# A planned kernel of attention and two feed-forward layers: strided masks on SyncE's queue, a planner that counts eight transfers, three more raw-weight buffers, other constants

## The chip, the cores and the metric

The program runs on one core of one Trainium2 chip. The metric is the device time of one execution in microseconds (us); the median of several runs is quoted. The profile below is of one further execution, which has a time of its own.

## The reference

Attention over 4 batches, 8 heads, 576 positions, head size 64. Heads 0 to 3 use a local mask (a window of 32), heads 4 to 7 a strided mask (every 32nd position). Its output, 2304 tokens by 512, goes through two feed-forward layers of width 2048, all in float32:

```python
mask_local = (rel >= 0) & (rel < stride)                          # stride 32
mask_strided = (rel >= 0) & (pos[None, :] % stride == pos[:, None] % stride)
scores = np.where(masks, scale * q @ k.T, -1e9)
attn = softmax(scores) @ v          # then (B*S, H*D) = (2304, 512)
h = x @ w_in;  g = h * np.clip(h + 3.0, 0.0, 6.0) / 6.0;  x = g @ w_out      # first layer
h = x @ w_in;  g = h * np.tanh(softplus(h));              x = g @ w_out      # second layer
```

The weights reach the chip as raw 64-bit words, from which the kernel makes float32.

## The kernel before

**Attention** goes by 16 pairs of heads (4 batches, 4 pairs). Of each pair a qk tile and a v tile are loaded. TensorE makes the scores (L609), DVE adds the mask out of `mk_loc` or `mk_str` (L622), and the softmax follows: maximum on DVE (L654), subtraction on DVE or POOL (L655), exponential on ACT (L656), sum on DVE (L657), a guard (L661 or L663), reciprocal (L666), and the scaling (L667). TensorE then transposes (L676, L678), ACT or DVE copies the result to `pt`, and TensorE makes the values (L715, 72 rows of the profile to a pass). Before that a part of v has been copied to other partitions (L575 on ACT). The first pairs use the late ends of the `xs` tiles as buffers, which is why some of their loads are named `xs`.

**The feed-forward layers** are matmuls of three products each, high and low parts of both operands (L1012 to L1014). Part of the first layer is done plainly, as soon as attention has some tokens ready; the rest, and most of the second, goes by a seven-product scheme in which sums and differences of blocks take the place of one product in eight.

**Weights** come as 64 loads of 512 KB into `raw` tiles (L793), each then turned into float32 by five DVE passes (L797 to L822, or L830 as the last), the first of which may run on ACT for the first 20. A raw tile is free again after the last pass. The differences of weight blocks (`w<-w`, L898) run on DVE or POOL; a split into high and low part follows (L348 on ACT or L350 on DVE, then L776 on DVE or POOL).

**The order** is not written by hand. Every step is an `Op` with its cost on each engine that may run it, the ops that it waits for, and a due time. `Plan.run` walks through an imagined time: it picks the op that can start first (among those within 11 ns the one due first), puts it on its engine, and at the end emits all ops by their imagined start. An op with two possible engines goes to that whose end, cost times `SLOW` plus `BIAS`, comes first. DVE and POOL shut each other out for the ops marked with `lock`. All loads and stores share one imagined engine `dma`, which does one transfer after another; its results count as there 2.1 us after the end. Where TensorE would stand still in the first 60 us of the plan, `fill` puts in matmuls on zeros (L1382, 512 columns of float32) whose results nobody reads. On the chip each engine runs its list in order and waits by semaphores; a filler that is in the list runs, whether the gap is there or not.

Loads and stores are issued on SyncE (SP), but for the seven loads of the strided masks, which are the first instructions on ScalarE's queue (L515). Of these, three bring rows that POOL or DVE then place in the strided mask (L532). `N_RAW` is 2: raw tile n is loaded when the unpacking of n - 2 is done (L788 and the load below it).

Of the kernel before, what the change touches and what calls it, by code (L numbers as in the profile page):

```python
# [10 lines left out]
U64 = mybir.dt.uint64  # L11
# [4 lines left out]
P = 128  # L16
# [39 lines left out]
N_KEEP = 2  # L56
N_RAW, N_WA, N_T, N_F = 2, 2, 3, 4
N_S = {"c": 2, "u": 2, "v": 2}
N_QKV, N_E, N_PT = 2, 4, 2

ABS_ON_ACT = 20
# [12 lines left out]
ORIGIN = 600  # L74
START, FIRST_PACE = 42920, 3359
UNIT = 858
MASKS_DUE = 1000
# [6 lines left out]
HALF_PACE = 4685  # L84
EARLY_W, EARLY_G, EARLY_X = 10496, 10545, 13159
OVERLAP = 14375
UNIT_Y, UNIT_X = 6429, 15237
LEAD = 1.0667


BIAS = {"act": -305, "dve": 318, "pool": 0}
FIRST_BIAS = {"act": -795, "dve": 929, "pool": -68}
BIAS_FROM = 17386

SLOW = {"pe": 1.0, "act": 1.04, "dve": 1.11, "pool": 0.95, "dma": 1.25}

# [38 lines left out]
class Plan:  # L135
# [84 lines left out]
    def run(self):  # L220
# [11 lines left out]
        done = []  # L232
        left = len(self.ops)
        while left:
            best = None
            for e, waiting in ready.items():
                mine = []
                for item in waiting:
                    r, op = item
# [3 lines left out]
                    t = at[e]  # L243
                    if e == "pe":
                        t += self.late(t, op)
                    if len(op.costs) > 1:
                        bias = BIAS if t > BIAS_FROM else FIRST_BIAS
                        end = {x: at[x] + c * SLOW[x] + bias[x] for x, c in op.costs.items()}
                        if min(end, key=end.get) != e:
                            continue  # L250
# [4 lines left out]
                t, due, item = min((x for x in mine if x[0] <= soon), key=lambda x: x[1])  # L255
# [10 lines left out]
            op.start, op.end = t, self.stream(t, op) if e == "pe" else t + op.cost * SLOW[e]  # L266
            free[e] = op.end
            if e == "pe":
                n = self.counted[-1][0]
                self.counted.extend([(n, t), (n + (op.count or 6), op.end)])  # L270
# [51 lines left out]
def attention_then_two_ffns(ctx, tc, qkv, masks, wts, out):  # L322
# [3 lines left out]
    nc = tc.nc  # L326
# [69 lines left out]
    zeros = spare[0][:, 2 * S:][:, :FILL]  # L396
    scratch = ap_.tile([P, 1], F32, name="scratch")

    def open_late():
# [86 lines left out]
    def load_masks(local):  # L486
# [26 lines left out]
        def load(rows, to, col, dims):  # L513
            src = bass.AP(tensor=masks.tensor, offset=masks.offset + n_mk + col, ap=[*dims, [row, QN], [1, WK]])
            return add("act", 430, lambda: nc.scalar.dma_start(to(rows), src), due=MASKS_DUE)  # L515

# [7 lines left out]
        for h in range(2):  # L524
            done.append(load(halves[h], lambda rows: mk_str[rows, 0], (NB - 1) * SK, [[QN * row + ODD_LAST, 2]]))
        done = [add("dma", 300, lambda: None, done)]
        odd = add("dma", 300, lambda: None, odd)

# [6 lines left out]
        for part in parts:  # L535
            done.append(add(None, {"dve": 200, "pool": 400}, lambda eng, part=part: place(eng, *part), [odd], lock=("dve",)))
        return done
# [226 lines left out]
    for k in halves[::-1]:  # L764
        t = h_due[k] = min(h_due[k] - EARLY_W, t - HALF_PACE)
    raw_ops, wa_ops, w32_ops = [], [], []
    in_use, out_use = {}, {}
# [14 lines left out]
    def unpack(m, fp, k, whole_tile):  # L782


        n = len(raw_ops)
        raw, a = raw_t[n % N_RAW], wa_t[n % N_WA]
        words = raw.bitcast(U32).rearrange("p (n t) -> p n t", t=2)
        low, high = words[:, :, 0], words[:, :, 1]  # L788
        ai = a.bitcast(U32)
        old = raw_ops[n - N_RAW] if n >= N_RAW else []  # L790
        old_a = wa_ops[n - N_WA] if n >= N_WA else []
# [27 lines left out]
        if whole_tile:  # L819
# [4 lines left out]
            )  # L824
            raw_ops.append([o])
            return o, a
        to = w32[:, 4 * (k % 2):][:, :4].bitcast(U32).rearrange("p b c -> p (b c)")
# [4 lines left out]
        )  # L832
        raw_ops.append([o])
        wa_ops.append([o])
        return o
# [622 lines left out]
```

## Time and profile before

| | us |
|---|---|
| median of 3 runs | 824.23 (824.16 to 824.65) |
| the profiled execution | 822.89 |
| its span, first to last instruction | 821.1 |
| busy: TensorE (PE) | 808.3 |
| busy: VectorE (DVE) | 676.0 |
| busy: ScalarE (ACT) | 447.2 |
| busy: GpSimd (POOL) | 325.9 |
| mean granted TensorE clock | 0.997 |

An engine's busy time is a share of the span; matmuls overlap each other in TensorE's pipeline, so that the sum of their durations is more than the busy time. Fillers count as busy. "SPq" and "ACTq" are the instructions by which SyncE and ScalarE issue transfers; they count as busy for no engine.

### The profile page before, as it was taken

How to read it: one execution, taken by the hardware profiler on the slowest of the kernel's cores; microseconds unless marked ns; L12 is line 12 of the kernel's file. 1: busy time of each engine (PE TensorE's matmuls, PEld its weight loads, DVE VectorE, ACT ScalarE, POOL GpSimd, SP SyncE). 2: the span in 40 equal slices, each digit the busy share in tenths (PEclk: the TensorE clock that was granted, in tenths of full speed). 3: DMA queues.
4: the chain of work that ended last, by engine and by line, in shares of the span. 5: the costliest groups of instructions: out<-in, count | busy, mean ns of one | idle time of the engine just before them, and what ended most of it. 6: DMA issues, size and time to landing. Idle time of an engine off the chain costs nothing.

```text
span 821.1 us, 17043 instructions
## 1 busy us (share of the span) xinstructions
PE 808.3 (98%) x6650; PEld 771.0 (94%) x6650; DVE 676.0 (82%) x1238; ACT 447.2 (54%) x941; POOL 325.9 (40%) x324
## 2 busy tenths in 40 slices
PE   6999999999999999999999999999999999999998
PEld 3678888899999999999999999999999999999998
DVE  4888887898999857867889899776888999998766
ACT  2767767666654434434436568556555545545542
POOL 4443421412252314231424324422677456476223
PEclk9999999999999999999999999999999999999999
DMA  8786751477678866765866446665667667765732
GB/s 241 229 248 184 211 178 54 146 303 268 249 251 297 295 251 238 263 226 184 288 219 229 184 168 268 225 239 196 241 240 244 225 212 244 247 237 188 246 126 96
DMA packets 47588, 182.31 MB, mean 222 GB/s; under 512 B 6036, under 2 KB 15380, under 8 KB 47508
## 3 DMA queue, kind: packets, MB, share of 16 engines
q1 hardware_dynamic: 46848, 181.06, 64.0%
q8 instruction: 52, 0.85, 0.4%
q10 hardware_dynamic: 660, 0.16, 0.1%
q14 instruction: 28, 0.23, 0.1%
HBM read 138.74 MB, written 42.47 MB: 221 GB/s over the span
## 4 chain that ended last, share of the span: by engine, by line
PE 89%; DVE 4%; DMA 3%; ACT 1%; POOL 1%; issue 1%; ACTq 0%; SPq 0%; DVEq 0%
PE bank L1012 29%; PE bank L1013 28%; PE bank L1014 28%; PE bank L715 2%; DMA raw<-in_wts_dram 1%; PE bank L609 1%; DMA v<-in_qkv_dram 1%; PE bank L676 1%; DMA mk_str<-in_masks_dram 1%; POOL w L898 1%; PE bank L1382 0%; DMA qk<-in_qkv_dram 0%; DVE wa L816 0%; DVE xs L1295 0%; DVE wa L811 0%
## 5 line engine op out<-in xcount | busy, mean ns | idle before, releaser
L1012 PE MATMUL bank<-x,win 128*128 128x384 f32 (+3 forms) x668 | 227.8, 341 | 0.4 <-POOL win L776 0.2
L1013 PE MATMUL bank<-x,win 128*128 128x384 f32 (+3 forms) x668 | 226.2, 339 | 0.1
L1014 PE MATMUL bank<-x,win 128*128 128x384 f32 (+3 forms) x668 | 226.1, 338 | 0.0
L1012 PE MATMUL bank<-g,wout 128*128 128x384 f32 (+3 forms) x512 | 175.7, 343 | 0.0
L1013 PE MATMUL bank<-g,wout 128*128 128x384 f32 (+3 forms) x512 | 174.2, 340 | 1.1 <-DVE g L776 1.1
L1014 PE MATMUL bank<-g,wout 128*128 128x384 f32 (+3 forms) x512 | 174.0, 340 | 0.0
L1295 DVE TENSOR_TENSOR xs<-bank,xs 128x384 f32<-128x384 f32 x174 | 95.2, 552 | 49.5 <-PE bank L1014 48.3
L1012 PEld LDWEIGHTS bank<-x,win 128*128 128x128 f32 x668 | 125.4, 188 | 5.3 <-POOL win L776 1.4
L1013 PEld LDWEIGHTS bank<-x,win 128*128 128x128 f32 x668 | 125.4, 188 | 2.8 <-POOL x L776 0.5
L1014 PEld LDWEIGHTS bank<-x,win 128*128 128x128 f32 x668 | 125.4, 188 | 2.2
L1013 PEld LDWEIGHTS bank<-g,wout 128*128 128x128 f32 x512 | 96.1, 188 | 3.0 <-DVE g L776 1.1
L1014 PEld LDWEIGHTS bank<-g,wout 128*128 128x128 f32 x512 | 96.1, 188 | 2.3
L1012 PEld LDWEIGHTS bank<-g,wout 128*128 128x128 f32 x512 | 96.1, 188 | 2.0
L898 POOL TENSOR_TENSOR w<-w 128x256 f32<-128x256 f32 x80 | 68.2, 871 | 70.1 <-DVE w L830 69.0
L1013 PE MATMUL bank<-g_late,wout 128*128 128x384 f32 x204 | 68.1, 334 | 0.0
L1012 PE MATMUL bank<-g_late,wout 128*128 128x384 f32 x204 | 68.1, 334 | 0.0
L1014 PE MATMUL bank<-g_late,wout 128*128 128x384 f32 x204 | 68.1, 334 | 0.0
L776 POOL TENSOR_TENSOR x<-xs,x 128x512 fp32r<-128x512 f32 (+3 forms) x17 | 21.1, 1244 | 63.7 <-ACT x L348 52.9
L816 DVE SCALAR_TENSOR_TENSOR wa<-raw,wa 128x512 uint32<-128x512 uint32 x64 | 45.8, 723 | 0.3
L776 POOL TENSOR_TENSOR win<-w,win 128x256 fp32r<-128x256 f32 (+1 forms) x25 | 29.1, 1170 | 40.6 <-ACT win L348 34.9
L348 ACT CAST win<-w 128x512 fp32r<-128x512 f32 (+1 forms) x56 | 31.6, 567 | 22.8 <-DVE w L830 14.6
L348 ACT COPY u<-bank 128x384 f32<-128x384 f32 x42 | 20.2, 482 | 37.6 <-PE bank L1014 37.4
(139 smaller groups left out, 1481.6 us busy)
## 6 DMA issues: line engine op xcount, KB each, us to landing
x<-kept_s SPq DMA_DIRECT2D x60, 768.0 KB, 4.4
x<-kept_a SPq DMA_DIRECT2D x45, 768.0 KB, 4.6
raw<-in_wts_dram SPq DMA_DIRECT2D x64, 512.0 KB, 5.0
kept_s<-x SPq DMA_DIRECT2D x24, 768.0 KB, 3.4
kept_a<-x SPq DMA_DIRECT2D x18, 768.0 KB, 4.0
qk<-in_qkv_dram SPq DMA_DIRECT2D x14, 576.0 KB, 5.3
v<-in_qkv_dram SPq DMA_DIRECT2D x14, 432.0 KB, 5.0
keep<-y SPq DMA_DIRECT2D x24, 192.0 KB, 4.1
```

Of the source, the lines that this page charges most:

```text
L348: nc.scalar.copy(out, src)
L609: nc.tensor.matmul(banks[both[h].n][g * QN:(g + 1) * QN, slot * WK:(slot + 1) * WK], src.q[h * D:(h + 1) * D, n // 6, n % 2 * QN:(n % 2 + ...
L676: nc.tensor.transpose(banks[turned[0].n][:, j * P:(j + 1) * P], e[:, t:t + 2].rearrange("p s k -> p (s k)"), ident)
L715: nc.tensor.matmul(o[h * D:(h + 1) * D], src.v[rows, NB + others(local).index(n) if n in others(local) else i, h * D:(h + 1) * D], pt[rows ...
L776: lambda eng: engines[eng].tensor_tensor(lo(), src(), hi().bitcast(F32), ALU.subtract),
L816: lambda: nc.vector.scalar_tensor_tensor(ai, high, 0xC0000000, ai, ALU.bitwise_and, ALU.bitwise_or),
L898: lambda eng: engines[eng].tensor_tensor(of[out], of[x], of[y], ALU.subtract), [*on[x], *on[y]], lock=("dve", "pool"),
L1012: nc.tensor.matmul(o, low_w, high, start=first, stop=False, skip_group_check=True)
L1013: nc.tensor.matmul(o, high_w, low, start=False, stop=False, skip_group_check=True)
L1014: nc.tensor.matmul(o, high_w, high, start=False, stop=last, skip_group_check=True)
L1295: "dve", dve_ns(n), lambda: nc.vector.tensor_tensor(y(), src(), y(), ALU.add), [prev, y_sums[key]], due=due, frees=frees,
```

## The change

Four edits. The seven loads of strided masks are issued by SyncE and planned on the `dma` engine. The planner lets a transfer start only when the eighth transfer before it has landed. Three more raw tiles serve weight loads number 2, 3, 4 and 7, so that of the first eight loads five need no freed tile. And a number of constants are others. The code's lines shift by 3 to 11 (L609 becomes L615, L715 becomes L721, L1382 becomes L1393, L898 becomes L909).

```diff
+N_RAW_MORE, RAW_EARLY = 3, 8
+LANES = 8
-START, FIRST_PACE = 42920, 3359
+START, FIRST_PACE = 42920, 3750
-EARLY_W, EARLY_G, EARLY_X = 10496, 10545, 13159
+EARLY_W, EARLY_G, EARLY_X = 10496, 10545, 11906
-UNIT_Y, UNIT_X = 6429, 15237
+UNIT_Y, UNIT_X = 5251, 15237
-BIAS = {"act": -305, "dve": 318, "pool": 0}
+BIAS = {"act": -305, "dve": 115, "pool": 45}
-SLOW = {"pe": 1.0, "act": 1.04, "dve": 1.11, "pool": 0.95, "dma": 1.25}
+SLOW = {"pe": 1.0, "act": 1.04, "dve": 1.11, "pool": 0.9037, "dma": 1.2274}
...
+                    elif e == "dma" and len(landed) >= LANES:
+                        t = max(t, landed[-LANES])
...
+            if e == "dma":
+                landed.append(op.end + self.AFTER[e])
...
+    raw_t.extend(ap_.tile([P, DM], U64, name=f"raw_more{k}") for k in range(N_RAW_MORE))
...
-            return add("act", 430, lambda: nc.scalar.dma_start(to(rows), src), due=MASKS_DUE)
+            return add("dma", 400, lambda: nc.sync.dma_start(to(rows), src), due=MASKS_DUE)
...
-        done = [add("dma", 300, lambda: None, done)]
-        odd = add("dma", 300, lambda: None, odd)
...
-        raw, a = raw_t[n % N_RAW], wa_t[n % N_WA]
+        slot = n % (N_RAW + N_RAW_MORE) if n < RAW_EARLY else n % N_RAW
+        raw, a = raw_t[slot], wa_t[n % N_WA]
...
-        old = raw_ops[n - N_RAW] if n >= N_RAW else []
+        old = raw_last.get(slot, [])
```

What this does to the order shows first on SyncE, at the very start of the program. The names are the tiles that are loaded: `mk` the local masks, `mk_str` and `mk_odd` the strided ones, then qk and v tiles of the first pairs. Before:

```order
L489 DMA mk<-in_masks_dram 128x320
L547 DMA qk_143<-in_qkv_dram 128x1152
L547 DMA qk_144<-in_qkv_dram 128x1152
L547 DMA xs_75<-in_qkv_dram 128x1152
L559 DMA v_145<-in_qkv_dram 96x1152
L547 DMA xs_76<-in_qkv_dram 128x1152
L559 DMA v_145<-in_qkv_dram 64x128
L793 DMA raw_79<-in_wts_dram 128x512
```

And now, on the same engine at the same place:

```order
L497 DMA mk<-in_masks_dram 128x320
L523 DMA mk_str<-in_masks_dram 128x1x64 x2
L523 DMA mk_odd<-in_masks_dram 64x1x64 x2
L523 DMA mk_odd<-in_masks_dram 128x1x64
L523 DMA mk_str<-in_masks_dram 64x1x64 x2
L553 DMA qk_143<-in_qkv_dram 128x1152
L553 DMA qk_144<-in_qkv_dram 128x1152
L553 DMA xs_75<-in_qkv_dram 128x1152
L565 DMA v_145<-in_qkv_dram 96x1152
L565 DMA v_145<-in_qkv_dram 64x128
L800 DMA raw_79<-in_wts_dram 128x512
```

Seven mask loads stand ahead of the first qk load; the order behind them is nearly the old one.

ScalarE at the start of the program, before (`e_147` and `e_148` are the scores of the first two pairs, `v_145` the first v tile, `sum_155` the first pair's sums):

```order
L515 DMA mk_str<-in_masks_dram 128x1x64 x2
L515 DMA mk_odd<-in_masks_dram 64x1x64 x2
L515 DMA mk_odd<-in_masks_dram 128x1x64
L515 DMA mk_str<-in_masks_dram 64x1x64 x2
L1381 ACT_TABLE_LOAD
L1381 ACTIVATE scratch<-xs_75 128x1
L656 ACTIVATE e_147<-e_147 128x320
L575 COPY v_145<-v_145 32x1024
L656 ACTIVATE e_147<-e_147 128x256
L661 ACTIVATE sum_155<-sum_155 128x5
```

And now:

```order
L1392 ACT_TABLE_LOAD
L1392 ACTIVATE scratch<-xs_75 128x1
L662 ACTIVATE e_147<-e_147 128x320
L662 ACTIVATE e_147<-e_147 128x256
L581 COPY v_145<-v_145 32x1024
L667 ACTIVATE sum_155<-sum_155 128x5
```

The issues are gone, and the second exponential of the first pair has moved ahead of the copy of v.

TensorE up to the first scores, before (fillers are the rows with 512 columns, `bank` is where a result goes):

```order
L1382 MATMUL bank_61<-xs_75 128x512
L1382 MATMUL bank_62<-xs_75 128x512
L609 MATMUL bank_63<-qk_143 32x64
L609 MATMUL bank_64<-qk_143 32x64
```

And now:

```order
L1393 MATMUL bank_61<-xs_75 128x512
L1393 MATMUL bank_62<-xs_75 128x512
L1393 MATMUL bank_63<-xs_75 128x512
L1393 MATMUL bank_64<-xs_75 128x512
L1393 MATMUL bank_65<-xs_75 128x512
L615 MATMUL bank_66<-qk_143 32x64
L615 MATMUL bank_67<-qk_143 32x64
```

Three more fillers stand ahead of the first scores. In the whole program 24 fillers stand where 17 did, all ahead of the sixth pass of values; by then 30 matmuls of 512 columns stand where 27 did, and seven passes of scores where eight did. Beyond the start, DVE has 104 instructions more (1344 for 1240) and POOL 89 fewer (240 for 329); 50 of the 80 differences `w<-w` are on DVE, where none was. By groups of four, those of the fourth group are all on DVE now, of the last group one.

## Rows read from the trace of the kernel before

**Rows 1.** Windows: length, busy time and instructions by engine, granted clock, transfers' share and GB/s.
```profile
0.00:52.50 52.50, 45.53 (x1065) 28.69 (x1065) 35.64 (x83) 31.96 (x68) 23.12 (x40) 0.97 0.80 237
52.50:60.00 7.50, 6.54 (x166) 5.34 (x166) 6.72 (x13) 3.15 (x7) 5.20 (x4) 1.00 0.82 242
60.00:140.00 80.00, 80.00 (x1558) 67.86 (x1557) 64.38 (x120) 56.21 (x116) 23.47 (x21) 1.00 0.55 167
```

**Rows 2.** Windows of 60 us; first engine PE, then PEld, DVE, ACT, POOL.
```profile
260.00:320.00 60.00, 59.80 (x344) 59.29 (x343) 46.70 (x87) 25.49 (x53) 16.98 (x16) 1.00 0.74 267
380.00:440.00 60.00, 60.00 (x348) 60.00 (x348) 53.06 (x99) 26.69 (x56) 22.04 (x23) 1.00 0.68 233
440.00:500.00 60.00, 59.19 (x342) 58.87 (x341) 51.96 (x96) 37.03 (x81) 20.95 (x20) 1.00 0.51 201
740.00:800.00 60.00, 59.49 (x342) 58.88 (x341) 44.01 (x82) 30.63 (x64) 22.83 (x22) 1.00 0.57 188
```

**Rows 3.** Timeline of PE: start, length, instruction, count, [idle before, and until what].
```profile
1.45 3.50 PE L1382 MATMUL bank<-xs 128*128 128x512 f32 x4 [1.45 <-DVE xs L1380]
5.72 1.05 PE L609 MATMUL bank<-qk 64*32 64x64 f32 x76 [0.77 <-DMA qk<-in_qkv_dram]
...
8.40 3.70 PE L1382 MATMUL bank<-xs 128*128 128x512 f32 x8
...
15.91 1.05 PE L609 MATMUL bank<-xs 64*32 64x64 f32 x76 [2.50 <-DMA xs<-in_qkv_dram]
...
19.00 4.04 PE L1382 MATMUL bank<-xs 128*128 128x512 f32 x6
...
52.50 0.90 PE L715 MATMUL bank<-pt,v 64*64 64x32 f32 x48
```

**Rows 4.** Groups by line, 0 to 60 us: the fillers; busy us, mean ns.
```profile
L1382 PE MATMUL bank<-xs 128*128 128x512 f32 x34 | 19.0, 692 | 1.5 <-DVE xs L1380 1.5
```

**Rows 5.** Timeline of the two issuing queues, 0 to 8 us.
```profile
0.73 1.77 ACTq L515 DMA_DIRECT2D mk_str<-in_masks_dram  x2
1.19 0.97 SPq L547 DMA_DIRECT2D qk<-in_qkv_dram  x2
2.53 1.68 ACTq L515 DMA_DIRECT2D mk_odd<-in_masks_dram  x3
5.09 1.88 ACTq L515 DMA_DIRECT2D mk_str<-in_masks_dram  x2
...
7.08 0.33 SPq L547 DMA_DIRECT2D xs<-in_qkv_dram  x1
...
7.45 0.43 SPq L559 DMA_DIRECT2D v<-in_qkv_dram  x1
```

**Rows 6.** Waits of SyncE's queue, 0 to 60 us: us in total, times, longest.
```profile
SPq L793 <- DVE wa L822: 16.8, 4, 7.6
...
SPq L547 <- DMA mk_str<-in_masks_dram: 4.9, 1, 4.9
```

**Rows 7.** Timelines of ACT and of DVE around 15 us.
```profile
14.45 1.04 ACT L575 COPY v<-v 32x1024 f32<-32x1024 f32 x1 [4.58 <-DMA v<-in_qkv_dram]
...
15.97 0.42 DVE L657 TENSOR_REDUCE sum<-e 128x4 f32<-128x256 f32 x1 [4.86 <-ACT e L656]
```

**Rows 8.** The page's queues: ScalarE's queue; packets, MB, share of 16 engines.
```profile
q10 hardware_dynamic: 660, 0.16, 0.1%
```

**Rows 9.** A window of 3 us; the granted clock is the third number from the end.
```profile
18.50:21.50 3.00, 3.00 (x6) 1.52 (x6) 1.66 (x8) 1.94 (x7) 1.87 (x2) 0.50 0.97 265
```

**Rows 10.** Groups by line: a difference on POOL, and a larger one on DVE.
```profile
L898 POOL TENSOR_TENSOR w<-w 128x256 f32<-128x256 f32 x80 | 68.2, 871 | 70.1 <-DVE w L830 69.0
...
L1237 DVE TENSOR_TENSOR f<-c,u 128x384 f32<-128x384 f32 x7 | 3.9, 557 | 3.0 <-ACT u L1153 3.0
```

**Rows 11.** The chain that ended last: start, us, what; two pieces ahead of late stalls.
```profile
263.83 1.45 POOL w L898 x2
...
743.63 2.97 POOL w L898 x3
```

More of the change, by code (lines that the diff above doesn't have):

```diff
@@ L232, in run @@
         done = []
-        left = len(self.ops)
+        left, landed = len(self.ops), []
         while left:
@@ L535, in load_masks @@
         for part in parts:
-            done.append(add(None, {"dve": 200, "pool": 400}, lambda eng, part=part: place(eng, *part), [odd], lock=("dve",)))
+            done.append(add(None, {"dve": 200, "pool": 400}, lambda eng, part=part: place(eng, *part), odd, lock=("dve",)))
         return done
@@ L765, in attention_then_two_ffns @@
         t = h_due[k] = min(h_due[k] - EARLY_W, t - HALF_PACE)
-    raw_ops, wa_ops, w32_ops = [], [], []
+    raw_ops, wa_ops, w32_ops, raw_last = [], [], [], {}
     in_use, out_use = {}, {}
@@ L825, in unpack @@
             raw_ops.append([o])
+            raw_last[slot] = [o]
+            if slot >= N_RAW:
+                closing.deps.append(o)
             return o, a
@@ L833, in unpack @@
         raw_ops.append([o])
+        raw_last[slot] = [o]
         wa_ops.append([o])
```

## The prediction

> **What bounds the kernel now.** I read the windows first. From 60 us on TensorE is busy throughout: 80.00 of 80.00 us between 60 and 140, and later 60.00 of 60 with 348 matmuls in a window, which is 0.172 us for each [rows 1, 2]. Three later windows hold 344, 342 and 342, so 4 + 6 + 6 = 16 matmuls are missing, and 16 x 0.172 = 2.76 us is all that TensorE loses there. Everything else is lost in the first 60 us: TensorE is busy 45.53 + 6.54 = 52.07 us, so it is idle 7.93 us, 1.45 of it before its first instruction [rows 1, 3]. And 19.0 us of what counts as busy is fillers, the matmuls on zeros of L1382: 34 rows, two to an instruction, so 17 [rows 4]. The time is therefore a fixed amount of matmul work, plus fillers, plus idle time. A faster DVE or POOL is worth nothing unless it removes one of these.
>
> Next I asked why TensorE has nothing to do early. SyncE issues two qk loads by 2.16 us and the next at 7.08; the queue's own waits put 4.9 us of that to a transfer of mk_str [rows 5, 6]. The seven strided-mask loads are ACT's first instructions and take it from 0.73 to 6.97 us. Since SyncE's third load waits for a mask that ScalarE issued, the two queues share a set of semaphores, which the built program's order of waits confirms (eight of them, used in turn). The load of v thus leaves at 7.45 us. ACT's copy of v stands ahead of the second exponential of the first pair; ACT waits 4.58 us for v, and DVE, which needs that exponential, 4.86 us [rows 7]. Later in the first 60 us SyncE stands four times, 16.8 us together, at a raw load whose buffer DVE hasn't freed [rows 6], and all loads behind it wait too.
>
> **The change, part by part.**
> *Masks on SyncE.* ACT loses 1.77 + 1.68 + 1.88 = 5.33 us of issuing. SyncE gains seven issues ahead of the first qk load, from 1.19 us on. What they cost there isn't shown; the bounds are SyncE's shortest row of one issue, 0.33, so 2.3 us, and ACT's 5.33 us [rows 5]. I take 0.45 each, 3.15 us, near SyncE's rows, 0.33 to 0.49. The mask issues would then end at 1.19 + 3.15 = 4.3, and qk leaves at 4.3 in place of 1.19. It lands 4.5 us after issue before (1.19 to 5.72, where TensorE waits for it [rows 3, 5]), so the first scores come at 8.8. Behind qk the 4.9 us wait is gone: the ninth transfer waits for the first one, which landed early. The load of v would leave near 5.8 in place of 7.45.
>
> All 16 transfer engines would need 0.1% of the span, 0.8 us, for the masks' queue [rows 8]. Before, those packets ran on ScalarE's queue beside qk. [...]
>
> *Order of ACT.* Both exponentials now stand ahead of the copy of v, so the stall of 4.86 us on DVE can't come from there again. What is late next is ACT's guard of the sums, which stands behind the copy; with v asked for 1.6 us sooner, that costs less than what was saved.
>
> *Eight transfers under way, and fillers.* The planner now sees loads arrive later, and fills the gaps that it sees: 24 fillers where 17 stood. A filler that stands in a gap costs nothing; one that stands where work is ready delays it. [...] So 24 cost 3.5 + 22 x 0.93 = 24.0 us if the clock doesn't fall again: 5.0 more than the 19.0. Five stand ahead of the first scores and end at 1.45 + 3.50 + 3 x 0.93 = 7.7, so those scores at 8.8 leave 1.1 us idle.
>
> *Three raw buffers.* The third to fifth weight loads need no freed buffer, and SyncE doesn't stand there. The 16.8 us of waiting was not TensorE's own, so I give it no sum of its own; it is why I expect little idle time besides that 1.1.
>
> *Constants.* On POOL the subtraction w (L898) occurs 80 times, 871 ns each; 50 of them move to DVE. DVE's nearest row is 128x384 at 557 ns, 1.5 times the size [rows 10], which is the upper bound; the lower is that in proportion, 371. I take 0.5 us, as fixed costs don't shrink. DVE gets 104 instructions in all, POOL 89 fewer. By 50 x 0.5 and 54 x about 0.6, DVE rises by some 57 us from 676.0 to about 733 of 821 us, and POOL falls by 50 x 0.87 and 39 x about 1.1, to some 240. Engines beside TensorE have that room on average. Two of the three late stalls end in chains with w on POOL: 1.45 us for two, 2.97 us for three [rows 11]. The first group of these is wholly on DVE now, so 1.45 becomes about 1.0; the last keeps three of its four on POOL. The third stall has none. Hence I keep 0.8 of the 2.76 us.
>
> **The sum**, against the profiled execution's own 822.89 us: fillers +5.0; the early idle time, 7.93 - 1.45 = 6.48, goes and 1.6 takes its place (the 1.1 and 0.5 more); late stalls -2.76 + 0.8. That is 5.0 - 6.48 + 1.6 - 2.76 + 0.8 = -1.84, so 821.1. The median of the runs shown, 824.23, is 1.34 above the profiled one, so the forecast is 822.4. In general the change is -4.24 plus the idle time that is left, early and late. With none left it is 820.0. With as much as before (6.48 + 2.76) it is +5.0, thus 829.2: if the plan fills gaps that then open all the same, its fillers are pure loss.
>
> **The rivals.**
> *Everything fits* (idle time 1.1 early and nothing late): -3.1, 821.1. For it: the stalls at 4.9 and 16.8 us of SyncE are real, and the planner now knows them. Against: seven places where a filler ended up in front of ready work need a plan exact to 0.9 us.
> *No change.* Early idle time 2.6, late stalls 1.8: +0.2, 824.4. The gaps only move, because the first scores start 3.1 us later; DVE, now at 733 us, makes new late stalls for those taken away. For it: the stall without w at 440 to 500 us, 6 matmuls, is made of x and g work on DVE, and DVE gets more of both. If the planner's picture of eight transfers isn't the chip's, the change doesn't do what it says, and the result lies here too.
> *Late first scores*, the one on the other side: seven mask issues on SyncE cost as on ACT, 5.33 us. Then qk leaves at 6.5 and lands at 11.0; TensorE has run out of fillers at 7.7, so the gap is 3.3 and not 1.1 us. An idle stretch of 2.50 us was followed by three fillers in 4.04, 1.25 more than 3 x 0.93 [rows 3]. The wait of 2.50 us for an xs load comes again, all transfers being late. 3.3 + 1.25 + 2.5 + 0.8 - 4.24 = +3.6, 827.8. From 5.9 us of idle time in all the kernel is slower by over 0.2%. For it: four of the loads are 128 short rows, and ACT took 0.89 us for one of the first pair. Against: SyncE's rows for 128 long ones are 0.33 to 0.49.
> [...]
>
> **How the numbers follow.** A difference under 0.2%, 1.65 us, can't be told from none, so faster means under 822.6 and slower above 825.9. Chances: the forecast 0.42 (of which 0.27 falls under 822.6), everything fits 0.20 (all faster), no change 0.20 (0.16 within, 0.03 slower, 0.01 faster), late first scores 0.18 (0.17 slower). That gives faster 0.48, same 0.32, slower 0.20. The range goes from 819.5, half a microsecond under the time with no idle left, for fillers that cost less than 0.93, to 826.3, which leaves out the worse half of the late case. The forecast's own range is 820.9 to 824.2.
>
> **What would show it.** SyncE's mask issues take about 3.2 us and the first qk leaves near 4.3; the first scores start near 8.8; no wait of SyncE for a mask; both exponentials run before the copy of v; DVE has no stall of 4 us there. Fillers: 48 rows, some 24 us. The sixth pass of the attention's values, which began at 52.50 [rows 3], begins near 53.3, 26.2 us of real work in front of it (45.53 - 19.0 = 26.5, less 0.3: three more 512-column matmuls at some 0.23, one pass of scores at 1.0 less), and behind it the 0.96 us idle of [rows 1] is gone. Late windows hold 348 matmuls but for one or two. It is wrong if the qk load leaves after 6 us, if fillers run while scores or values are ready, or if DVE's late chains are longer than before.

## The result and the profile after

The median of six runs is 830.46 us (829.68 to 832.0); the kernel before, on the same chip, took 824.19 (823.6 to 824.66). The ratio is 1.0078, with an interval from 1.0065 to 1.0091: slower by 0.8%, clear of the runs' scatter, and outside the predicted range of 819.5 to 826.3. The profiled execution took 830.47 us, its span is 828.7, which is 7.6 more than the span before, and the mean granted clock is 0.995.

From the windows of the kernel after (busy time and instructions of PE, PEld, DVE, ACT, POOL, then granted clock, transfers' share, GB/s):

```profile
0.00:52.50 52.50, 41.70 (x828) 25.28 (x829) 30.26 (x73) 24.82 (x53) 14.83 (x29) 0.93 0.79 225
52.50:60.00 7.50, 7.50 (x168) 5.40 (x167) 5.76 (x12) 5.51 (x12) 2.74 (x3) 1.00 0.51 146
60.00:140.00 80.00, 79.58 (x1621) 65.87 (x1619) 70.14 (x133) 53.95 (x108) 25.39 (x20) 1.00 0.59 183
...
260.00:320.00 60.00, 60.00 (x348) 59.92 (x347) 46.57 (x95) 24.66 (x52) 10.03 (x8) 1.00 0.77 282
...
440.00:500.00 60.00, 60.00 (x348) 60.00 (x347) 55.13 (x108) 36.16 (x78) 20.01 (x14) 1.00 0.50 196
740.00:800.00 60.00, 60.00 (x346) 59.75 (x346) 48.04 (x88) 28.26 (x61) 21.67 (x20) 1.00 0.61 204
```

Beside [rows 1, 2]: the late windows now hold 348, 348 and 346 matmuls where they held 344, 342 and 342. The first 60 us hold 49.20 us of busy TensorE where they held 52.07. So the loss is early, and late there is a gain.

TensorE's timeline, to be held against [rows 3] (start, length, instruction, count, idle before and what ended it):

```profile
1.45 6.42 PE L1393 MATMUL bank<-xs 128*128 128x512 f32 x10 [1.45 <-DVE xs L1391]
9.29 1.05 PE L615 MATMUL bank<-qk 64*32 64x64 f32 x76 [1.42 <-DMA qk<-in_qkv_dram]
...
15.94 0.77 PE L615 MATMUL bank<-xs 64*32 64x64 f32 x51
17.39 0.46 PE L615 MATMUL bank<-xs 64*32 64x64 f32 x25 [0.68 <-issue]
...
23.03 0.42 PE L721 MATMUL bank<-pt,v 64*64 64x32 f32 x13
27.88 1.92 PE L721 MATMUL bank<-pt,v 64*64 64x32 f32 x59 [4.42 <-issue]
...
41.71 1.03 PE L615 MATMUL bank<-qk 64*32 64x64 f32 x74
44.46 0.27 PE L615 MATMUL bank<-qk 64*32 64x64 f32 x2 [1.71 <-issue]
...
62.81 1.25 PE L721 MATMUL bank<-pt,v 64*64 64x32 f32 x72
```

Three times TensorE stops in the middle of a pass: after 51 of 76 rows, 13 of 72, 74 of 76. "issue" says that the engine waited for nothing that the profile shows. Before there was one such wait in the first 60 us, of 0.96 us, in the sixth pass of values:

```profile
54.36 0.55 PE L715 MATMUL bank<-pt,v 64*64 64x32 f32 x24 [0.96 <-issue]
```

That pass begins at 62.81 where it began at 52.50; 53.3 was forecast.

All that TensorE waits for in the first 60 us of the kernel after (us in total, times, longest):

```profile
PE bank L721 <- issue: 4.4, 1, 4.4
PE bank L615 <- issue: 2.4, 2, 1.7
PE bank L1393 <- DVE xs L1391: 1.5, 1, 1.5
PE bank L615 <- DMA qk<-in_qkv_dram: 1.4, 1, 1.4
PE bank L682 <- DVE e L673: 0.7, 1, 0.7
PE bank L682 <- ACT pt L355: 0.4, 1, 0.4
```

Without the 1.45 us before the first instruction 9.3 us of idle time are left, 6.8 of them named issue. The fillers, from the groups by line of the same stretch, and the window behind the longest of these waits:

```profile
L1393 PE MATMUL bank<-xs 128*128 128x512 f32 x48 | 25.5, 662 | 1.5 <-DVE xs L1391 1.5
```

```profile
25.70:32.50 6.80, 4.62 (x67) 3.45 (x66) 0.29 (x2) 2.12 (x8) 0.00 (x0) 0.50 1.03 294
```

The granted clock is 0.50 from 25.7 to 32.5 us, from within the idle 4.42 us (23.45 to 27.88) on; TensorE is busy for 4.62 us there, and a filler pair took 1.77.

**The whole 7.6 us.** TensorE is busy 814.0 us where it was 808.3: +5.7, of which the fillers are +6.5 (25.5 for 19.0) and the rest -0.8. Its idle time is 828.7 - 814.0 = 14.7 where it was 821.1 - 808.3 = 12.8: +1.9, made of 10.80 - 7.93 = +2.9 in the first 60 us and -1.0 behind them.

SyncE's issues at the start, which answer to [rows 5], and its longest waits from 0 to 60 us, which answer to [rows 6]:

```profile
1.18 1.33 SPq L523 DMA_DIRECT2D mk_str<-in_masks_dram  x2
2.55 1.68 SPq L523 DMA_DIRECT2D mk_odd<-in_masks_dram  x3
4.27 1.06 SPq L523 DMA_DIRECT2D mk_str<-in_masks_dram  x2
5.38 0.91 SPq L553 DMA_DIRECT2D qk<-in_qkv_dram  x2
```

```profile
SPq L565 <- PE bank L721: 16.8, 3, 9.0
SPq L553 <- PE bank L615: 10.9, 3, 7.1
```

Seven mask issues take 4.07 us, 0.58 each. SyncE no longer waits for masks or raw tiles. It waits as long for TensorE's passes, which free the tiles of the next qk and v loads.

The start of ACT and DVE, which answers to [rows 7], and the differences of weights, which answer to [rows 10]:

```profile
12.90 0.99 ACT L662 ACTIVATE e<-e 128x320 f32<-128x320 f32 x2 [10.67 <-POOL e L661]
14.83 1.04 ACT L581 COPY v<-v 32x1024 f32<-32x1024 f32 x1 [0.94 <-DMA v<-in_qkv_dram]
...
16.13 0.27 DVE L672 RECIPROCAL sum<-sum 128x5 f32<-128x5 f32 x2 [1.08 <-ACT sum L667]
```

```profile
L909 POOL TENSOR_TENSOR w<-w 128x256 f32<-128x256 f32 x30 | 26.9, 905 | 32.1 <-DVE w L840 29.9 <-DVE w L909 2.0
L909 DVE TENSOR_TENSOR w<-w 128x256 f32<-128x256 f32 x50 | 24.2, 512 | 0.1
```

The softmax chain runs as forecast: both exponentials ahead of the copy of v, a DVE stall of 1.08 us where 4.86 stood. DVE is busy 706.1 us, POOL 254.1.

**What "issue" is here.** The page's queue table has this line (packets, MB, share of 16 engines), so 16 KB a packet:

```profile
q8 instruction: 52, 0.85, 0.4%
```

One of them lies in the longest wait (the same, window 23.4 to 26.5):

```profile
q8 instruction: 1, 0.02, 2.4%
```

It begins at 25.04 us, ends at 26.25, and TensorE goes on at 27.88. 6664 matmuls and as many weight loads over 52 packets are 256.3 to a packet; whose instructions a packet holds, no record shows. The planner of both kernels holds a model in blocks of 256, which the prediction doesn't use: the line `PIECE, ASKED, AHEAD, SUPPLY = 256, 140, 308, 6000` lets a block of 256 begin at the 448th instruction of TensorE, the 704th and so on, and has it there 6.0 us after the instruction 308 places ahead of it was begun. On the chip the 198th matmul, at which the count of 396 is reached, begins at 16.16 us, and TensorE goes on at 27.88 from the stop at 699 of its records, the one nearest to the 704th: 11.7 us. The theory that I took to the experiments (A), an estimate from that 256.3 and the model, which no record shows by itself: TensorE's instructions come in blocks of 256, the stops are where a block runs out before the next is there, and the blocks are late because data is ahead of them. The rivals: the fillers and the late first scores cost the time (B), or the constants do (C), or any other order of the start brings its own accidents (D).

### The profile page after: what moved, and what is told of

It is laid out like the page before. It is cut to its first block, busy times and chain, and to the rows that moved or that the text cites. A ratio compares the mean times of both kernels' runs of the same rounds, so it can differ in the third digit from the quotient of the medians.

```text
span 828.7 us, 17086 instructions
## 1 busy us (share of the span) xinstructions
PE 814.0 (98%) x6664; PEld 774.8 (93%) x6664; DVE 706.1 (85%) x1342; ACT 441.2 (53%) x926; POOL 254.1 (31%) x235
## 4 chain that ended last, share of the span: by engine, by line
PE 93%; DVE 3%; issue 1%; ACT 1%; SPq 1%; POOL 0%; DMA 0%; POOLq 0%
PE bank L1023 29%; PE bank L1025 29%; PE bank L1024 29%; PE bank L721 2%; PE bank L615 2%; PE bank L1393 1%; PE bank L682 1%; SPq L523 0%; DMA qk<-in_qkv_dram 0%; PE bank L684 0%; DVE win L782 0%; DVE xs L1306 0%; DVE wa L818 0%; POOL g L782 0%; DVE w L909 0%
## 5 line engine op out<-in xcount | busy, mean ns | idle before, releaser
L782 POOL TENSOR_TENSOR win<-w,win 128x512 fp32r<-128x512 f32 (+1 forms) x21 | 27.3, 1305 | 54.2 <-ACT win L355 52.4
L823 DVE SCALAR_TENSOR_TENSOR wa<-raw,wa 128x512 uint32<-128x512 uint32 x60 | 43.4, 727 | 0.2
L355 ACT CAST win<-w 128x512 fp32r<-128x512 f32 (+1 forms) x54 | 30.1, 568 | 19.1 <-DVE w L840 13.2
L355 ACT COPY u<-bank 128x384 f32<-128x384 f32 x42 | 20.2, 482 | 36.7 <-PE bank L1025 36.6
L355 ACT COPY xs<-bank 128x288 f32<-128x288 f32 (+1 forms) x56 | 23.0, 442 | 30.2 <-PE bank L1025 17.1
```

The source lines that it names most:

```text
L355: nc.scalar.copy(out, src)
L782: lambda eng: engines[eng].tensor_tensor(lo(), src(), hi().bitcast(F32), ALU.subtract),
L823: lambda: nc.vector.scalar_tensor_tensor(ai, high, 0xC0000000, ai, ALU.bitwise_and, ALU.bitwise_or),
```

## The experiments

All ratios are to the kernel before, run on the same chip between the others. The profiled executions lie within 2.7 us of the medians, but for those of u_masks (841.82) and o_const (827.35).

**1. One part of the change at a time.** u_masks puts the masks back on ScalarE, in the plan too:

```diff
-            return add("dma", 400, lambda: nc.sync.dma_start(to(rows), src), due=MASKS_DUE)
+            return add("act", 430, lambda: nc.scalar.dma_start(to(rows), src), due=MASKS_DUE)
```

> The change with the seven mask loads back on ScalarE's queue and in its plan; all else as changed; the planner's order is made anew (18 fillers). Theory A (TensorE's instruction blocks come too late where attention passes follow each other closely, which the late first scores bring about): first scores near 5.7 us, issue waits of TensorE in the first 60 us under 1.5 us in total (6.8 in the changed kernel), time 822 to 826. Rival B (the seven more fillers are the loss): 1 filler more than before, about 825. Rival C (constants and DVE's work): stays near 830.

Measured 835.84, ratio 1.0158 (1.0116 to 1.0201), outside all three theories: the first scores do begin at 5.34 us, but the waits called issue are 5.4 us in the first 60, and 7.8 us are lost from 60 to 140. u_const has the old constants and all else changed:

> The change with the old constants (paces, EARLY_X, UNIT_Y, BIAS, SLOW); masks on SyncE, counting of eight transfers and raw buffers kept; 20 fillers, five of them ahead of the first scores as in the changed kernel. Theory A: the start is as late and as dense, an issue wait of 3 us or more stays, time 827 to 831. Rival B (fillers): 3 more than before at 0.93, about 827. Rival C (constants): back to 822 to 825.

832.74, 1.0110 (1.0094 to 1.0125), 1.7 us above theory A's range, with 5.6 us of issue waits in three pieces of at most 2.4. o_masks is the kernel before with the masks on SyncE alone:

> The kernel before with nothing but the masks' loads issued by SyncE and planned there; 21 fillers. Theory A: first scores near 9.3, issue waits of 3 us or more in the first 60 us, time 827 to 831. Rival B (fillers): 4 more at 0.93, about 828, and no long issue wait. Rival C (constants): 823 to 825.

839.14, 1.0188 (1.0171 to 1.0206), outside all three, with 2.2 us of issue waits. u_lanes takes out the count of eight transfers (`LANES = 10 ** 6`), u_raw the three buffers (`N_RAW_MORE = 0`), o_const is the kernel before with the new constants:

> The changed kernel with the plan's count of eight transfers under way taken out (LANES without a limit), all else as changed; 24 fillers per bank pair in the plan's order as in the changed kernel. Theory A: TensorE's start is the same and the instruction blocks come as late, so issue waits of 5 to 8 us remain in the first 60 us and the time is 828 to 833. Theory C (the count makes the plan put work where it does not fit): the loss goes, 822 to 826.

> The changed kernel without the three more raw buffers (two again). SyncE then waits for raw buffers early, so fewer transfers are under way at once between 5 and 30 us. Theory A: the second and third instruction block end earlier (by 1 to 4 us), the issue waits fall from 6.8 to 3 to 5 us, and the time to 824 to 828. Theory C (the order alone decides): any issue waits stay as they are, 829 to 832.

> The kernel before with the refitted constants alone (masks on ScalarE, two raw buffers, no count of transfers). The refit is what takes the late stalls away (after 140 us), as the changed kernel with old constants keeps them: theory A expects the late 2.8 us gone here too, and the first 60 us to be decided by another order of the start, 818 to 830, by whether a wait called issue of over 2 us stands there. Theory D (the refit is worth nothing on its own): 823 to 826, late stalls as before.

831.25, 1.0091 (1.006 to 1.0122); 842.85, 1.0227 (1.0195 to 1.0259); 832.49, 1.0095 (1.0063 to 1.0127). Of these six only u_lanes came out as theory A had it. No part does well alone, and none can be taken out with profit: what the parts are worth can't be added up, since each gives the planner another order of the start. u_raw went against theory A, which gave 824 to 828: its wait in the first pass of values is 4.7 us, and it loses another 8 us between 60 and 140 us. Two windows recur, here in o_masks (old constants) and in o_const (new ones):

```profile
60.00:140.00 80.00, 74.74 (x1498) 1.00 0.59 178
300.00:800.00 500.00, 498.47 (x2872) 1.00 0.66 229
```

```profile
60.00:140.00 80.00, 77.92 (x1605) 1.00 0.59 178
300.00:800.00 500.00, 500.00 (x2886) 1.00 0.66 225
```

With old constants TensorE loses 1.3 to 1.5 us from 300 to 800 us (before and u_const: 498.68), with new ones next to nothing (the changed kernel: 499.91). And in four of these orders 2 to 8 us more are lost between 60 and 140 us; why, no run here takes apart.

**2. The queue by itself.** d_masks keeps every engine's order of the changed kernel and issues the same seven loads on ScalarE's queue (`nc.scalar.dma_start` in place of `nc.sync.dma_start`).

> The changed kernel, every engine's order kept; only the queue that issues the seven mask transfers goes back from SyncE's to ScalarE's. Theory A (TensorE waits for its own instruction blocks, which arrive late beside the data): the first qk is issued near 1.2 us again instead of 5.4 and the first scores begin where the 16 fillers before them end, near 7.7 instead of 9.3, so at most 1.6 us come back there; the data goes out no later, so the waits called issue in the first values pass stay above 3 us, and the time is 827 to 830. Theory B (it is the late first qk that costs): the waits shrink with it and the time falls by over 4, to 824 to 826. Theory C (constants and order alone): no change, 830.

829.11, 1.0071 (1.0044 to 1.0099): in time as theory A has it. The first qk leaves at 1.19 us and no gap stands ahead of the first scores, yet TensorE waits in the first 60 us for:

```profile
PE bank L721 <- issue: 4.8, 3, 2.1
PE bank L615 <- issue: 2.3, 1, 2.3
```

That is as much in all as in the changed kernel, but the wait in the first pass of values is 1.96 us and not over 3: the rest has moved to later passes. The four stops stand at 698, 953, 1207 and 1462 matmuls and weight loads, 254 or 255 apart; the one stop of the kernel before, of 0.96 us, stands at 2227, six steps of 255 behind 697. By the medians the late first qk is worth 1.4 us at most; the intervals of the two ratios overlap.

**3. The fillers.** d_nofill keeps the order and puts no filler in (`lambda n: None` as what a filler does).

> The changed kernel, order kept, without the 48 filler products (they compute nothing that is kept). Theory B (25.5 us of fillers, which the plan puts where it believes TensorE idle, delay the work): the passes begin earlier and the time falls by 4 or more, to 822 to 826. Theory A (instruction blocks late): the 48 fillers and their weight loads also leave the instruction stream, so each block reaches further into the work by some 96 instructions; the wait of 4.4 in the first values pass falls under 2, but gaps stand where the fillers stood, the clock is low (0.50) in them, and the time is 829 to 836.

830.11, 1.0086 (1.0053 to 1.0119). Without 25.5 us of fillers the kernel takes the same time. Theory B falls: the fillers stand where TensorE would wait anyway. Theory A had the time right and the wait wrong: it was to fall under 2 us and is 4.60. Where it waits is told by counting; two windows of the changed kernel, then of d_nofill, that end in the first two stops:

```profile
0.00:17.00 17.00, 13.84 (x223) 6.74 (x223) 6.33 (x22) 4.52 (x9) 5.56 (x20) 1.00 0.71 230
0.00:27.00 27.00, 19.46 (x349) 9.96 (x350) 13.06 (x40) 8.50 (x18) 8.71 (x24) 0.98 0.84 238
```

```profile
0.00:18.00 18.00, 4.10 (x223) 3.40 (x223) 6.34 (x22) 4.74 (x9) 6.26 (x21) 1.00 0.74 235
0.00:27.50 27.50, 8.77 (x349) 6.91 (x350) 13.26 (x40) 8.51 (x18) 8.67 (x24) 1.00 0.84 242
```

Matmuls and weight loads: 223 and 223 at the first stop, 349 and 350 at the second, in both, though other work stands there. In d_nofill the second stop falls 39 rows into a pass of values, not 13:

```profile
22.09 1.28 PE L721 MATMUL bank<-pt,v 64*64 64x32 f32 x39
27.98 1.08 PE L721 MATMUL bank<-pt,v 64*64 64x32 f32 x33 [4.60 <-issue]
```

**4. Moving the stop.** d_pad20 and d_pad40 add small products of zeros behind the fifth filler, order kept:

```diff
+    pad = lambda n: [nc.tensor.matmul(banks[n][:w, :c], zeros[:, :w], zeros[:, :c], start=True, stop=True) for w, c in [(P, FILL)] + [(32, 64)] * 20]
```

> The changed kernel, order kept, with 20 small products of zeros (about 80 more TensorE instructions, 0.5 us, no result kept) behind the five fillers that stand ahead of the first scores, where TensorE has 1.4 us of idle. In five kernels so far TensorE stopped at the same count of its instructions (699 or 700 by the records), whatever work stood there. Theory A (the stops belong to blocks of 256 instructions that are fetched as TensorE gets on, 7 to 10 us each here): the stop moves 80 instructions back in the work, from inside the pass of values to the end of the scores ahead of it, the fetch is asked for before the wait for data at 12.7 to 16.1 us and not behind it, the wait called issue in the pass of values is under 2.5 us in place of 4.4, and the time is 826 to 829. Theory B (the wait is a hidden wait for data of the values): the stop stays at the 13th of 72 rows of that pass, 4 us or more, time 830 to 831.

> As the kernel with 20 small products, with 40 (about 160 more instructions, 1.1 us, still inside the idle 1.4 us). Theory A: the stop that was inside the pass of values lies near instruction 540 of the old count, at 20.3 us, and is short, since its block was asked for near 12 us; the first of the stops comes earlier too (near 11.9 us) and may cost up to 1 us; time 825 to 829. Theory B: as the changed kernel, 830 to 832.

834.26, 1.0134 (1.0115 to 1.0153), and 833.56, 1.0122 (1.0107 to 1.0137). In the timeline of d_pad20 the stop has left the pass of values and stands in the scores ahead of it, at 350 matmuls again:

```profile
21.12 0.81 PE L615 MATMUL bank<-xs 64*32 64x64 f32 x54
26.58 0.66 PE L615 MATMUL bank<-xs 64*32 64x64 f32 x22 [4.65 <-issue]
```

So the stop belongs to the count, and it isn't a wait for the data of that pass. What I expected of its length was wrong: it didn't shrink. With 40 there is no stop at this count: the first one takes 3.04 us, the eight filler rows behind it take 5.40 us where eight took 3.70 (granted clock 0.67 from 18.56 to 23.74 us), and TensorE gets to its 349th matmul at 27.71, when the packet of 23.74 us is in. And the pads cost more than I allowed: with 40 the first scores come at 12.68 us, 3.4 later than without. In both kernels the packet begins 5.2 to 5.7 us after TensorE has gone on from the stop before (its 224th matmul). When a block is asked for, no record shows.

**5. Is the packet late because of the data?** d_light and d_light8 load 64 of 512 columns in the first four and eight raw loads, in the changed kernel's order; the rest of the tiles is preset, so the output is another.

```diff
+        cols = DM // 8 if n < 8 else DM
+        load = add("dma", dma_ns(8 * P * DM), lambda: nc.sync.dma_start(raw[:, :cols], wts[m, f, half][:, :cols]), old)
```

> The changed kernel with its order kept; of the first four raw weight loads only 64 of 512 columns are loaded (the rest of those tiles is set to ones by POOL at the start), 1.8 MB less in the first 30 us; the results of those weights are wrong. Theory A (instruction blocks wait behind the data transfers): the wait of 4.4 us in the first pass of values falls under 1.5 us, the block that came at 25.0 us comes before 22, time 821 to 826. Rival B (fillers): 24 fillers as before, 829 to 831. Rival D (blocks take a fixed time after they are asked for, whatever the transfers do): the wait stays above 3.5 us, time 828 to 831.

> The changed kernel, order kept; the first eight raw loads bring 64 of 512 columns (the rest of the tiles is preset by GpSimd; the output is another). Theory A (instruction packets wait behind data): the third packet (at 25.04 us in the changed kernel, 22.9 or so with four light loads) begins at 20 to 23 us, the wait in the first pass of values falls under 2 us, the later waits called issue fall too, and the time is 823 to 828. Theory B (the order alone decides): the packet and the wait stay as in the kernel with four light loads, 2.0 us, and the time is 829 or more.

829.14, 1.0066 (1.005 to 1.0083), and 827.08, 1.003 (1.0008 to 1.0052). The packet begins at 22.8 us in both, 2.2 earlier than in the changed kernel, and the wait in the first pass of values falls from 4.42 us to 2.03 (d_light, two rows) and 2.49 (d_light8, the third):

```profile
23.01 0.42 PE L721 MATMUL bank<-pt,v 64*64 64x32 f32 x13
25.47 1.72 PE L721 MATMUL bank<-pt,v 64*64 64x32 f32 x59 [2.03 <-issue]
...
25.68 1.12 PE L721 MATMUL bank<-pt,v 64*64 64x32 f32 x59 [2.49 <-issue]
```

For d_light that lies between what theories A (under 1.5) and D (over 3.5) expected, and its time can't be told from the changed kernel's. For d_light8 packet and time are where theory A had them, the wait is not (under 2). Its issue waits in the first 60 us are 2.9 us where the changed kernel has 6.8, and by the ratios it is some 4 us faster. The profiled executions of the two are 2.6 and 2.4 us faster than the medians.

o_heavy goes the other way: three more loads of 512 KB, into tiles that nobody reads, in the order of the kernel before.

```diff
+        load = add("dma", dma_ns(8 * P * DM), lambda: [nc.sync.dma_start(x, wts[m, f, half]) for x in [raw] + extra_t * (n == 1)], old)
```

> The kernel before, order kept, with three more loads of 512 KB (into tiles that nobody reads) on SyncE's queue behind the second raw load at 12 us. Theory A: 1.5 MB more at the 290 GB/s of this stretch keep the transfers busy 5 us longer; the packet at 18.39 us begins at 20.5 to 25 us, TensorE stops at its 700th instruction (none in the kernel before), and the time rises by 3 to 8, to 827 to 832. Theory B: the packet comes 8 us behind the one before it as in the kernel before (18 to 19.5 us), no wait called issue over 1 us before 30 us; the time rises only by waits for data, 824 to 828.

826.49, 1.0023 (1.0001 to 1.0046). The packet begins at 17.76 us (18.39 before), 5.2 us behind the 224th matmul (5.4 before), and no stop follows; the time is lost in waits for data. Here theory B of that run holds. So heavier loads added nothing. How far a packet scatters by itself is seen in three kernels of experiment 7, whose start is that of the kernel before: it begins 4.1 to 4.6 us behind the 224th matmul there, against the 5.4 of the kernel before itself. The 2.2 us of the lighter loads are more than these 1.3, but the packet is as early with full loads in d_masks (5.4 us behind the 224th matmul), d_pad20 and d_pad40. That data ahead of it delays the packet, the second half of theory A, is therefore not shown.

**6. Telling the plan.** u_supply8 and o_supply8 give the planner a delay of 8.8 us a block where it had 6.0, in the changed kernel and in the one before:

```diff
-PIECE, ASKED, AHEAD, SUPPLY = 256, 140, 308, 6000
+PIECE, ASKED, AHEAD, SUPPLY = 256, 192, 256, 8800
```

> The changed kernel, its plan told that a block of 256 TensorE instructions is asked for when the block before it is begun and takes 8.8 us (6 us and an earlier request in the changed kernel). Theory A: the waits called issue stay (the plan can't take them away), but what the plan puts around them fits; 823 to 829. Theory D (another order, another accident): 830 to 840.

> The same two numbers in the plan of the kernel before. Theory A: no loss against the kernel before, 820 to 825. Theory D: another order of the start and other accidents, 827 to 838.

870.99, 1.0563 (1.052 to 1.0607), and 872.28, 1.0585 (1.0536 to 1.0634): outside all that I expected. u_supply8 has only 0.6 us of issue waits in its first 60 us, and loses later:

```profile
60.00:140.00 80.00, 68.04 (x1314) 0.84 0.49 149
140.00:300.00 160.00, 148.52 (x1311) 0.94 0.53 184
```

It waits there for the softmax and its copies: from 60 to 300 us 6.2 us for the scaling (L673) and 4.2 for the masks (L628) on DVE, 4.8 for ACT's copies to `pt` and 4.5 for those to `xs` (L355). One number doesn't fit all packets: in the kernel before, two end as little as 3.8 us apart (30.8 and 34.6 us), two others 8.3 (11.33 and 19.65). That a plan which takes 8.8 us for each puts attention's many small products off is my reading; no run shows it by itself.

**7. The late part alone.** o_late uses the new biases and speeds for what the plan puts behind 60 us, o_late140 and o_late300 behind 140 and 300 us (the edit shown is o_late300's). `UNIT_Y`, the due time of the sums, is the new one in the whole plan; even so TensorE's order, by line and tile, is that of the kernel before up to 71.9 us in o_late, up to 162.8 in o_late140, and for its first 3000 matmuls in o_late300.

```diff
-UNIT_Y, UNIT_X = 6429, 15237
+UNIT_Y, UNIT_X = 5251, 15237
...
+LATE_FROM, LATE_BIAS, LATE_SLOW = 300000, {"act": -305, "dve": 115, "pool": 45}, {"pe": 1.0, "act": 1.04, "dve": 1.11, "pool": 0.9037, "dma": 1.2274}
...
-                        bias = BIAS if t > BIAS_FROM else FIRST_BIAS
+                        bias = (LATE_BIAS if t > LATE_FROM else BIAS) if t > BIAS_FROM else FIRST_BIAS
```

> The kernel before with the refitted biases, speeds and the due time of the sums (UNIT_Y) used only for work that the plan puts after 60 us; the order of the first 50 us is that of before. Theory A (the refit is good late, all the loss is in the first 60 us): the waits from 60 us on fall from 2.8 to under 1.2 us, time 821 to 823. Theory D (the gain late needs the other parts too): 824 to 827.

> The kernel before with the refitted biases, speeds and due time of the sums only for work that the plan puts after 140 us; the order before that is that of before. Theory A (the refit takes the late waits of 2.8 us away, the loss of the changed kernel is all in its first 60 us): TensorE busy 499.9 or more of the 500 us from 300 to 800 (498.68 before), 820.5 to 822.8, ratio below 0.999. Theory D (the late waits come from elsewhere and move on): 823 to 826.

> The same from 300 us of the plan on. Theory A: the waits after 300 us go (1.3 us by the busy time), 821.5 to 823.2. Theory D: 823 to 826.

o_late: 830.3, 1.0087 (1.0058 to 1.0116), outside both theories; 74.59 of the 80 us from 60 to 140 are busy, so its new order of attention's rest loses 5.4 us there, behind a start that is the old one. o_late140: 821.45, 0.9967 (0.9954 to 0.9979). o_late300: 820.84, 0.9957 (0.9941 to 0.9972). These two beat both kernels, by 0.3 and 0.4% of the one before. Windows of o_late300:

```profile
60.00:140.00 80.00, 80.00 (x1557) 1.00 0.58 174
...
440.00:500.00 60.00, 60.00 (x348) 1.00 0.51 202
740.00:800.00 60.00, 60.00 (x348) 1.00 0.57 191
```

The late stalls of [rows 2] behind 300 us, 6 matmuls each, are gone, and nothing is lost early. The profiled spans are 819.5 (o_late140) and 819.6 for 821.1, so 1.5 to 1.6 us by the spans of one execution each, and 2.5 to 3.2 by the medians.

## Why the prediction was wrong

**The step that failed** is "the early idle time, 7.93 - 1.45 = 6.48, goes and 1.6 takes its place (the 1.1 and 0.5 more)". 9.3 us took its place. The 1.1 is right as far as it goes: the gap ahead of the first scores is 1.42. The 0.5 more was 7.9, and 6.8 of that is the waits named issue, which the prediction didn't have among its rivals. It had one sign of it, the 0.96 us idle behind 52.50, and counted that as gone. None of its own three signs of being wrong came: qk left at 5.38 us, d_nofill shows no loss by fillers, and the late stalls are fewer.

**Why that wait appears.** Between the first and the second of the counts at which the changed kernel stops (its 224th and 350th matmul) the kernel before takes 10.3 us, 3.3 of it idle in waits for data and other engines, 2.50 us in one piece [rows 3]. The packet begins 5.4 us after the first count (18.39 us), so that TensorE, by an estimate from the 2.4 to 2.9 us seen below, could go on at 7.8 to 8.3 us, 2 us or more before it gets there. Without its waits it would need 7.0 us, an estimate from these rows, and would stop too. The change took most of the waits for data away: the same count of instructions is done in 6.06 us (17.39 to 23.45), and the packet, now 7.65 us after the first count, is followed by TensorE 2.84 us later. 7.65 + 2.84 - 6.06 = 4.43, the gap in front of the 27.88 us row. By the traces the packet began 3.8 to 8.1 us after that count in the kernels run; in the ten that stopped at the second count, TensorE went on 2.4 to 2.9 us after the packet had begun. In those ten the stretch took 7.4 us (o_masks) to 10.8 (u_raw), and what the work needs less than that turns into this wait. That the stop goes by count is shown (experiments 2 to 4); that TensorE is out of instructions there is my reading of the packets' times, and no record shows it. Why the packet is 2 us later in the changed kernel than in d_masks, which has nearly the same loads under way, stays open, and with it whether the 2.2 us of the lighter loads come from the loads. Nor has any run the changed order without these stops, so that they alone make the time of 830.46 is not shown; d_light8, with 3.9 us less of them and some 4 us less of time, comes nearest.

**The fillers** cost 25.5 us, not 24.0. The sum's 3.5 for the first two and 0.93 for each other are those of [rows 3], where four took 3.70 at a granted clock of 1.00. That step holds in the changed kernel where the granted clock is 1.00 (3.60 and 3.70 for four), but a pair that stood alone took 1.02 to 1.12 there, and one behind the 4.42 us wait took 1.77 from 31.05 us on, at a granted 0.50 up to 32.5; in the kernel before, the three of 4.04 us ran mostly at 0.50 too [rows 3, 9]. The prediction's sentence "With as much as before (6.48 + 2.76) it is +5.0, thus 829.2: if the plan fills gaps that then open all the same, its fillers are pure loss." comes nearest in number: idle time did open all the same. Put into its sum, the measured terms are 6.5 for the fillers, 10.80 - 7.93 = +2.9 for early idle time, -1.0 for late idle time and -0.8 of other busy time: +7.6. But the fillers are no loss of their own: taken out in d_nofill, they leave idle time in their place.

**Masks on SyncE.** 0.58 each, not 0.45, so that qk left at 5.38 and not 4.3; first scores at 9.29, forecast 8.8. It landed 3.9 us after its issue, no later than the 4.5 before: the masks' 640 packets of 256 bytes run from 2.71 us to 6.79, and the first of qk's packets of 4608 bytes starts at 6.43, 1.05 us after its issue (1.23 before), when all but 48 of them have started. The rival of late first scores had the right side and, at 827.8, somewhat over half of the size, but for a wrong reason: d_masks has no late first scores and can't be told from the changed kernel in time.

**SyncE's raw waits** went, as forecast; giving them no sum of their own was right. Waits of 16.8 us for TensorE's passes stand there now.

**ACT's order** came out as forecast, and so did the end of DVE's 4.86 us stall.

**The constants** did late what was forecast: DVE took 512 ns for a difference of weights (0.5 taken), it is busy for 706 us (733), POOL for 254 (240), and the stalls in the three windows fell from 16 matmuls to two. Of the forecast -2.0 us the changed kernel has -1.0 behind 60 us, since 0.4 is lost anew from 60 to 140 us; o_late140 and o_late300 show the part by itself, -1.6 and -1.5 by the spans. The 2.76 us that the prediction put on the late stalls, by missing matmuls, was the larger of two measures: by busy time the three windows of [rows 2] are idle 0.20 + 0.81 + 0.51 = 1.52 us. The forecast was the sum of a gain late that is there and a start that lost what it was to gain.

## What to carry to other kernels

Where the trace has a wait called issue, however short, count the instructions between such places, and look for the instruction queue's packets: in the ten kernels that stopped, a stretch of 253 matmuls and weight loads, most of them small, took 7.4 us or more, and waits for data may be hiding such a stop. Where the code holds a model of such a wait, hold its figure against the trace. A planner's order is one thing: a part of a change can't be priced by itself where it re-orders the start, so change constants only for the stretch in which the stalls stand. And a filler costs nothing only where the gap would be there without it; the kernel without fillers tells.

## What the runs showed of the hardware that was not expected

TensorE stopped at the same count of its records (698 to 700 matmuls and weight loads together) in ten of the kernels run, for 1.7 to 4.7 us (in an eleventh, u_supply8, for 0.64 us). Each time a 16 KB packet on the queue named instruction had begun 2.4 to 2.9 us before it went on, and in the changed kernel it had ended 1.6 us before. The packet itself took 1.1 to 1.3 us; between the first count and its start the transfers' share was 1.03 to 1.06 in all ten. Three loads of 512 KB added to the transfers (o_heavy) didn't delay it beyond its scatter (5.2 us behind the 224th matmul, 4.1 to 5.4 in the kernels with the same start). In the changed kernel the seven mask loads issued on SyncE took 0.58 us each, the two qk loads behind them 0.46.
